# Spectral layer and MLP on one core: where the temporary of the last two conversion steps of w_in lies

## The chip, the cores and the metric

The kernel runs on one core of a Trainium2 chip. The metric is the device time of one execution in microseconds (us), the median of several runs. Before the change it is 2545.39 us, the median of 3 runs (2545.13 to 2547.89).

## The reference

Each of 8 sequences of 3008 tokens with 256 features is taken to the frequency domain, multiplied by a complex 256x256 matrix with a bias, soft-thresholded and taken back. The 24064 tokens that result go through an MLP with 2048 hidden features. The weights `w_in` and `w_out` come in float64.

```python
X = np.fft.rfft(x, axis=1)
Yr = Xr @ w_r - Xi @ w_i + b_r
Yi = Xr @ w_i + Xi @ w_r + b_i
Y = sign(Y) * maximum(abs(Y) - 0.01, 0)      # for Yr and Yi apart
x = np.fft.irfft(Yr + 1j * Yi, n=3008, axis=1)
h = x @ w_in
out = np.maximum(0.01 * h, h) @ w_out
```

## The kernel before, in words

The transform of 3008 points is split into 47 x 64. Four stages do the spectral layer of one sequence:

- `fwd` (stage A): the transform over 47. Its results go to DRAM (`u_dram`). For the second sequence its matmuls are `psh<-xin` (L310 to L311) and its copies `xin<-psh` (L313).
- `mid`: twelve rounds, one for each pair of rows of the first transform, called round 0 to round 11 below. A round loads `u` (L357), makes the transform over 64 (`stage_b`, PE `psh<-fb,u`, L371), copies it (ACT `ef<-psh`, L375; DVE adds real and imaginary part, L376), multiplies by the complex matrix in three products (`proj`: PE `pso<-w,ef` and `psf<-w,ef`), adds the bias (DVE `kb`, L409, and `t<-psf,kb`, L417), thresholds (DVE L418, L419), puts the halves in place (four ACT or DVE rows `zf<-t`, L423 to L427), transforms back over 64 (`stage_g`, PE `psh<-zf`, L442), copies (`v`, L450) and writes to DRAM (`v_dram`, L452).
- `inverse`: the transform back over 47. It loads the tile `vin` (tag `vin`, two slots of 240 KB loads in pairs, L495). Each of four calls for the first block of tokens (two pairs of sets x two halves of the features) makes four products into one of two PSUM banks `psf` (PE `psf<-ga,vin`, L516); ACT copies half of the result (`odd`, L519) and DVE makes the tokens (L520, L522), and ACT puts them in the token tile `yc` (L529).
- `forms` splits the tokens of a block of 512 into high and low parts (`yh`, `yl`, L542, L543) for fp32r products.

The MLP runs over 47 blocks of 512 tokens and 8 steps each: `psh<-yh,win` products (L98), a leaky ReLU, and `pso<-gh,wout` products (L644). From the first block's MLP on, the spectral stages of later sequences run between the MLP's matmuls. The prelude is what stands before that: stages A and mid of the first sequence, stage A of the second, the conversion of `w_in` and the start of that of `w_out`.

`convert_win(c)` turns one quarter of `w_in` from float64 into a high and a low fp32r part, with four sums for a Strassen form. `float64_parts` (L148) makes q and a from the raw words: ACT L153 writes `cvq`, ACT L154 writes `cva`, and DVE rows L155 to L159 finish the two; L184 adds them. L187 to L190 make the sums `ws`; ACT L193 and DVE L194 write `win_hi` and `win_lo` in three pieces each. The raw words of quarters 0 and 1 lie in the place of tag `wout_hi`, those of 2 and 3 in that of `wout_lo`, since `w_out`'s own tiles of these tags come only after the last quarter. The tiles `a`, `q`, `s` (`win_tmp`, L739 to L742) serve all four quarters; `a` is in a slot of tag `vin`, `q` of `gf`, `s` of `yh`.

A call of `convert_win` gives its instructions to a scheduler, which sets the order on each engine by a timeline of its own, within the `issue_after` ties that the code gives. Quarter 2 is converted after the third sixteenth of mid (L763), quarter 3 after the last threshold (L770). Each engine takes its instructions in the order that the scheduler wrote, and the SP queue likewise takes its DMA issues.

Of the kernel before, what the change touches and what calls it, by code (L numbers as in the profile page):

```python
# [8 lines left out]
F32 = mybir.dt.float32  # L9
# [11 lines left out]
P = 128  # L21
# [10 lines left out]
def spectral_mlp_kernel(  # L32
# [23 lines left out]
    NH = D // P  # L56
# [13 lines left out]
    sb = ctx.enter_context(tc.tile_pool(name="sb", bufs=2))  # L70
# [77 lines left out]
    def float64_parts(raw, a, q):  # L148


        wl, wh = raw[:, :, 0], raw[:, :, 1]
        u = a.bitcast(U32)
        act.mul(q, wl, 2.0 ** -52)  # L153
        act.activation(a, wh.bitcast(F32), AF.Abs, scale=2.0 ** 16)  # L154
        dve.tensor_scalar(a, a, F64_MIN * 2.0 ** 16, F64_MAX * 2.0 ** 16, ALU.max, ALU.min)  # L155
        dve.tensor_scalar(u, u, 4, 1, ALU.logical_shift_left, ALU.logical_shift_right)
        dve.scalar_tensor_tensor(u, wh, 0x80000000, u, ALU.bitwise_and, ALU.bitwise_or)
        dve.tensor_scalar(wl, u, 0xFF800000, None, ALU.bitwise_and)
        dve.tensor_mul(q, q, wl.bitcast(F32))  # L159
# [5 lines left out]
    NIN = DF // 4  # L165
# [13 lines left out]
    def convert_win(c):  # L179


        a, q, s = win_tmp
        float64_parts(win_raw[c], a, q)
        dve.tensor_add(a, a, q)  # L184
        a = a.rearrange("p (j q i m) -> p j q i m", j=NH, q=2, i=2)
        a11, a12, a21, a22 = (a[:, j, :, i] for i in range(2) for j in range(2))
        dve.tensor_add(s[:, 0], a21, a22)  # L187
        dve.tensor_sub(s[:, 2], a11, a21)
        dve.tensor_sub(s[:, 1], s[:, 0], a11)
        dve.tensor_sub(s[:, 3], a12, s[:, 1])  # L190
        hi, lo = (w[:, :, 2 * c:2 * c + 2] for w in consts["win"])
        for k, w in ((slice(0, 2), a[:, :, :, 0]), (2, a22), (slice(3, 7), s)):
            act.copy(hi[:, k], w)  # L193
            last = dve.tensor_sub(lo[:, k], w, hi[:, k].bitcast(F32))  # L194
        return last
# [528 lines left out]
    for h in range(2):  # L724
# [16 lines left out]
        sb.tile([P, NH * NIN], F32, name="cva", tag="vin"), sb.tile([P, NH * NIN], F32, name="cvq", tag="gf"),  # L741
        sb.tile([P, 4, 2, P], F32, name="ws", tag="yh"))  # L742
    convert_win(0)
    with tc.issue_after(turned[0].ins):
        split_consts()
# [12 lines left out]
    with tc.issue_after(turned[0].ins):  # L758
        convert_win(1)
    wout = load_wout()  # L760
    for i in range(1, 17):
        m0.to(i / 16)
        if i == 3:  # L763
            convert_win(2)
        if 5 <= i < 12:
            next(fp)
        if i == 13:
            next(wout)
# [146 lines left out]
```

## Time and profile before

| what | value |
|---|---|
| median of 3 runs | 2545.39 us (2545.13 to 2547.89) |
| the profiled execution | 2545.12 us, of which its span 2543.3 us |
| busy PE / DVE / ACT in the span | 98% / 74% / 66% |
| mean granted TensorE clock | 0.995 |
| first matmul of the MLP | 119.75 us from the span's start |

A row of the timeline gives the start and the length in us from the span's start, the engine, the line, output and input tiles, the shapes, and how many instructions are merged; the bracket says how long the engine sat idle before and what it waited for. One float32 product shows as two PE records. The length of a row is that of its results; the next row on an engine can start a little before it ends, so steps below are taken from start to start. SPq and ACTq rows are DMA issues.

### The profile page before, as it was taken

How to read it: one execution, taken by the hardware profiler on the slowest of the kernel's cores; microseconds unless marked ns; L12 is line 12 of the kernel's file. 1: busy time of each engine (PE TensorE's matmuls, PEld its weight loads, DVE VectorE, ACT ScalarE, POOL GpSimd, SP SyncE). 2: the span in 40 equal slices, each digit the busy share in tenths (PEclk: the TensorE clock that was granted, in tenths of full speed). 3: DMA queues.
4: the chain of work that ended last, by engine and by line, in shares of the span. 5: the costliest groups of instructions: out<-in, count | busy, mean ns of one | idle time of the engine just before them, and what ended most of it. 6: DMA issues, size and time to landing. Idle time of an engine off the chain costs nothing.

```text
span 2543.3 us, 42385 instructions
## 1 busy us (share of the span) xinstructions
PE 2500.5 (98%) x16180; PEld 2251.0 (89%) x16180; DVE 1877.5 (74%) x3460; ACT 1675.1 (66%) x3152; POOL 116.9 (5%) x96
## 2 busy tenths in 40 slices
PE   6999999999999999999999999999999999999999
PEld 4688889999899998999989999899998998999998
DVE  7887778777877778777786777877778776766675
ACT  4776756677666765677656677567765676666564
POOL 0000000000000000000000000000000000000000
PEclk8999999999999999999999999999999999999999
DMA  8621132111421113221141211411114111100000
GB/s 268 195 80 50 45 92 84 46 53 38 113 63 42 54 38 110 58 58 43 41 118 50 58 42 38 123 57 54 37 35 134 50 50 42 44 21 29 10 17 17
DMA packets 117803, 165.05 MB, mean 65 GB/s; under 512 B 13513, under 2 KB 69345, under 8 KB 117601
## 3 DMA queue, kind: packets, MB, share of 16 engines
q1 hardware_dynamic: 76228, 112.34, 14.5%
q10 hardware_dynamic: 41373, 50.01, 7.6%
q8 instruction: 127, 2.08, 0.3%
q14 instruction: 75, 0.61, 0.1%
HBM read 86.59 MB, written 75.71 MB: 64 GB/s over the span
## 4 chain that ended last, share of the span: by engine, by line
PE 92%; DVE 3%; DMA 2%; ACT 2%; issue 1%; ACTq 0%; SPq 0%; DVEq 0%
PE pso L644 39%; PE psh L98 35%; PE psf L84 11%; PE psf L516 4%; PE psf L371 3%; DMA xin<-x_dram 1%; DMA u_dram<-xin 1%; DVE gl L597 0%; PE psh L84 0%; PE psh L371 0%; PE pso L84 0%; DVE gf L628 0%; DMA win_raw<-w_in_dram 0%; DVE xz L279 0%; DMA vin<-v_dram 0%
## 5 line engine op out<-in xcount | busy, mean ns | idle before, releaser
L98 PE MATMUL psh<-yh,win_hi 128*128 128x256 f32 (+1 forms) x2608 | 736.5, 283 | 2.6 <-DVE gf L628 2.2
L98 PE MATMUL psh<-yl,win_hi 128*128 128x256 f32 (+1 forms) x2608 | 729.3, 280 | 0.0
L98 PE MATMUL psh<-yh,win_lo 128*128 128x256 f32 (+1 forms) x2608 | 726.6, 280 | 0.0
L597 DVE TENSOR_TENSOR gl<-gf,gh 128x1024 fp32r<-128x1024 f32 x376 | 460.8, 1226 | 323.8 <-ACT gh L595 315.8
L644 PE MATMUL pso<-gl,wout_hi 128*128 128x512 f32 x1504 | 590.6, 393 | 1.8 <-DVE gl L597 1.7
L644 PE MATMUL pso<-gh,wout_hi 128*128 128x512 f32 x1504 | 590.2, 392 | 1.1 <-ACT gh L595 1.1
L644 PE MATMUL pso<-gh,wout_lo 128*128 128x512 f32 x1504 | 589.7, 392 | 0.0
L98 PEld LDWEIGHTS psh<-yh,win_hi 128*128 128x128 f32 x2608 | 489.9, 188 | 20.5 <-DVE gf L628 4.6
L98 PEld LDWEIGHTS psh<-yl,win_hi 128*128 128x128 f32 x2608 | 491.0, 188 | 16.4 <-DVE yl L543 0.3
L98 PEld LDWEIGHTS psh<-yh,win_lo 128*128 128x128 f32 x2608 | 489.9, 188 | 2.1
L595 ACT CAST gh<-gf 128x1024 fp32r<-128x1024 f32 x376 | 394.8, 1050 | 43.7 <-PE pso L644 30.8
L631 ACT ACTIVATE gf<-gf 128x768 f32<-128x768 f32 x368 | 311.8, 847 | 153.7 <-DVE gf L628 140.3
L644 PEld LDWEIGHTS pso<-gl,wout_hi 128*128 128x128 f32 x1504 | 283.0, 188 | 61.7 <-DVE gl L597 3.8
L644 PEld LDWEIGHTS pso<-gh,wout_hi 128*128 128x128 f32 x1504 | 283.0, 188 | 46.3 <-ACT gh L595 1.9
L644 PEld LDWEIGHTS pso<-gh,wout_lo 128*128 128x128 f32 x1504 | 282.8, 188 | 45.5
L630 ACT ACTIVATE gf<-psh 128x256 f32<-128x256 f32 x368 | 142.2, 386 | 239.3 <-PE psh L98 233.5
L628 DVE TENSOR_TENSOR gf<-psh,u 128x512 f32<-128x512 f32 x368 | 252.0, 685 | 25.6 <-PE psh L98 24.1
L612 ACT COPY p<-psh 128x256 f32<-128x256 f32 x368 | 136.9, 372 | 147.5 <-PE psh L98 140.0
L409 POOL TENSOR_TENSOR kb<-bias,kc 128x512 f32<-128x512 f32 x84 | 114.3, 1360 | 2056.8 <-ACT kc L407 1804.2
L613 DVE TENSOR_TENSOR u<-psh,p 128x256 f32<-128x256 f32 x368 | 154.2, 419 | 70.6 <-ACT p L612 69.6
L615 DVE TENSOR_TENSOR gf<-psh,u 128x256 f32<-128x256 f32 x368 | 154.3, 419 | 29.3 <-PE psh L98 15.4
L616 DVE TENSOR_TENSOR gf<-psh,gf 128x256 f32<-128x256 f32 x368 | 154.1, 419 | 5.3
(124 smaller groups left out, 3153.5 us busy)
## 6 DMA issues: line engine op xcount, KB each, us to landing
u<-u_dram SPq DMA_DIRECT2D x192, 128.0 KB, 2.7
v_dram<-v ACTq DMA_DIRECT2D x192, 128.0 KB, 2.4
out_dram<-ob SPq DMA_DIRECT2D x94, 256.0 KB, 2.0
vin<-v_dram SPq DMA_DIRECT2D x96, 240.0 KB, 3.6
xin<-x_dram SPq DMA_DIRECT2D x78, 240.0 KB, 3.0
u_dram<-xin ACTq DMA_DIRECT2D x72, 240.0 KB, 2.4
raw<-w_out_dram SPq DMA_DIRECT2D x8, 512.0 KB, 4.8
win_raw<-w_in_dram SPq DMA_DIRECT2D x7, 512.0 KB, 6.8
```

The lines of the kernel that those rows point to most:

```text
L84: last = nc.tensor.matmul(dst, a, b, start=(i == 0), stop=(i == len(terms) - 1))
L98: mlp[:] = [nc.tensor.matmul(dst, a, b, start=start and i == 0, stop=i == 2, skip_group_check=True)]
L595: cp = act.copy(gh, g)
L597: parted[:] = [cp, dve.tensor_sub(gl, g, gh.bitcast(F32))]
L612: act.copy(p1, b1[:, lo])
L613: dve.tensor_add(u2, b1[:, hi], p1)
L615: dve.tensor_add(g[:, 3], b2[:, hi], u2)
L616: dve.tensor_add(g[:, 3], b2[:, lo], g[:, 3])
L628: dve.tensor_add(g[:, 1:3], b2.rearrange("p (k n) -> p k n", k=2), u2.unsqueeze(1).broadcast_to([P, 2, HT]))
L630: act.activation(g[:, 0], b1[:, lo], AF.Prelu, alpha=SLOPE)
L631: act.activation(g[:, 1:4], g[:, 1:4], AF.Prelu, alpha=SLOPE)
L644: mlp[:] = [nc.tensor.matmul(po, a[:, f, s], r[:, i], start=(f == 0 and j == 0), stop=(f == NF - 1 and j == 2),)]
```

## The change

For quarters 2 and 3 the temporary `a` is a new tile in the place of tag `wout_hi`, which held the raw words of quarters 0 and 1. The slot of tag `vin` holds `a` for quarters 0 and 1 only.

```diff
         a, q, s = win_tmp
+        if c >= 2:
+            a = sb.tile([P, NH * NIN], F32, name="cva", tag="wout_hi", bufs=1)
         float64_parts(win_raw[c], a, q)
```

No instruction is added or removed, but the scheduler puts many in another order. All lines below L181 have two more in the changed kernel (L371 is L373 there). The number behind a name tells tiles of one name apart.

On PE, in mid, after the third round's product with the sum (`pso_345`, round 2), before:

```order
L84 MATMUL pso_345<-w32_105,ef_229 128x256 x2
L84 MATMUL psf_346<-w32_105,ef_229 128x256 x4
L371 MATMUL psh_338<-fb_103,u_277 128x2x64 x4
L84 MATMUL psh_382<-zf_230,w32_105 128x512
L371 MATMUL psh_391<-fb_103,u_306 128x2x64 x4
L84 MATMUL psf_399<-w32_105,ef_229 128x256 x4
L84 MATMUL pso_398<-w32_105,ef_229 128x256 x2
L84 MATMUL psh_417<-zf_230,w32_105 128x512
```

The same place now:

```order
L84 MATMUL pso_345<-w32_105,ef_229 128x256 x2
L373 MATMUL psh_338<-fb_103,u_277 128x2x64 x4
L84 MATMUL psf_346<-w32_105,ef_229 128x256 x4
L84 MATMUL pso_399<-w32_105,ef_229 128x256 x2
L84 MATMUL psf_400<-w32_105,ef_229 128x256 x4
L84 MATMUL psh_383<-zf_230,w32_105 128x512
L373 MATMUL psh_392<-fb_103,u_306 128x2x64 x4
L84 MATMUL psh_418<-zf_230,w32_105 128x512
```

The transform of round 3 (`psh_338`) has moved ahead of the `psf` products of round 2, and both projections of round 3 ahead of the first `psh<-zf`.

On DVE, at the same time, between quarter 1's sums and the second `t` row (`t_297` is round 0, `t_326` round 1, `cva_180` the old temporary), before:

```order
L417 TENSOR_TENSOR t_297<-psf_288,kb_291 128x512
L194 TENSOR_TENSOR win_lo_179<-cva_180,win_hi_178 128x2x256
L194 TENSOR_TENSOR win_lo_179<-cva_180,win_hi_178 128x256
L189 TENSOR_TENSOR ws_182<-ws_182,cva_180 128x256
L418 TENSOR_SCALAR c_298<-t_297 128x512
L409 TENSOR_TENSOR kb_320<-bias_248,pso_316 128x512
L190 TENSOR_TENSOR ws_182<-cva_180,ws_182 128x256
L419 TENSOR_TENSOR t_297<-t_297,c_298 128x512
L417 TENSOR_TENSOR t_326<-psf_317,kb_320 128x512
```

And now (`cva_351` is the new temporary, quarter 2):

```order
L155 TENSOR_SCALAR cva_351<-cva_351 128x1024
L419 TENSOR_TENSOR t_297<-psf_288,kb_291 128x512
L196 TENSOR_TENSOR win_lo_179<-cva_180,win_hi_178 128x2x256
L196 TENSOR_TENSOR win_lo_179<-cva_180,win_hi_178 128x256
L191 TENSOR_TENSOR ws_182<-ws_182,cva_180 128x256
L156 TENSOR_SCALAR cva_351<-cva_351 128x1024
L420 TENSOR_SCALAR c_298<-t_297 128x512
L411 TENSOR_TENSOR kb_320<-bias_248,pso_316 128x512
L192 TENSOR_TENSOR ws_182<-cva_180,ws_182 128x256
L378 TENSOR_TENSOR ef_229<-ef_229 128x2x128
L157 SCALAR_TENSOR_TENSOR cva_351<-win_raw_251,cva_351 128x1024
L421 TENSOR_TENSOR t_297<-t_297,c_298 128x512
```

Three rows of quarter 2 and round 3's `ef` row have come ahead of round 0's threshold row (L419 before, L421 now). On ACT, `cva<-win_raw_251` of quarter 2 (L154) now stands directly behind round 2's `ef` copy, ahead of quarter 1's `win_hi` casts; before it came after all three of these.

On ACT, where the last of the four inverse calls is read out (`odd_828` before), before:

```order
L313 COPY xin_557<-psh_835 96x512
L529 COPY yc_797<-y_818 128x470
L519 COPY odd_828<-psf_823 128x240
L313 COPY xin_557<-psh_838 96x512
L313 COPY xin_557<-psh_841 96x512
```

And now (`odd_830`):

```order
L315 COPY xin_558<-psh_837 96x512
L315 COPY xin_558<-psh_840 96x512
L531 COPY yc_799<-y_820 128x470
L521 COPY odd_830<-psf_825 128x240
L315 COPY xin_558<-psh_843 96x512
```

The last `odd` row has gone from behind one to behind two of the three last copies of stage A.

On the SP queue, the four `vin` loads of the first block stood in the order pair 0, 0, 1, 1; now it is 0, 1, 0, 1, followed as before by two loads of `w_out`.

## The prediction

> **What bounds the kernel now.** I read the page first, then the busy time by stretches.
>
> ```profile
> span 2543.3 us, 42385 instructions
> PE 2500.5 (98%) x16180; PEld 2251.0 (89%) x16180; DVE 1877.5 (74%) x3460; ACT 1675.1 (66%) x3152; POOL 116.9 (5%) x96
> PE 92%; DVE 3%; DMA 2%; ACT 2%; issue 1%; ACTq 0%; SPq 0%; DVEq 0%
> ...
> 160.00:2543.00 2383.00, 2368.31 (x15649) 2157.21 (x15647) 1751.54 (x3244) 1569.77 (x2957) 116.11 (x90) 1.00 0.20 56
> ```
>
> PE bounds it: 42.8 us of the span are idle on PE, and only 14.7 of these come after 160 us. The other 28 lie in the prelude, which is what the change touches. After the prelude a shift of PE's start is carried to the end, since PE has next to no idle time there to take it up.
>
> The timeline of PE in mid, where the order changes, comes next:
>
> ```profile
> 48.18 1.89 PE L84 MATMUL psf<-w,ef 128*128 128x256 f32 x8
> 50.94 1.16 PE L371 MATMUL psh<-fb,u 128*128 128x128 f32 x8 [0.87 <-DMA u<-u_dram]
> 53.69 1.13 PE L84 MATMUL psh<-zf,w 128*128 128x512 f32 x2 [1.60 <-ACT zf L427]
> ...
> 55.55 1.89 PE L84 MATMUL psf<-w,ef 128*128 128x256 f32 x8
> 57.28 1.03 PE L84 MATMUL pso<-w,ef 128*128 128x256 f32 x4
> 58.14 1.02 PE L84 MATMUL psh<-zf,w 128*128 128x512 f32 x2
> 59.00 1.05 PE L371 MATMUL psh<-fb,u 128*128 128x128 f32 x8
> ...
> 67.27 1.10 PE L84 MATMUL pso<-w,ef 128*128 128x256 f32 x4 [1.15 <-DVE ef L376]
> ```
>
> Round 3's transform (50.94) waits for its load of `u`. While that load is on its way PE does round 2's `psf` products (48.18). The other two waits are for ACT and DVE, which are both full here. DVE and then ACT over the same time:
>
> ```profile
> 46.54 0.68 DVE L417 TENSOR_TENSOR t<-psf,kb 128x512 f32<-128x512 f32 x1
> ...
> 49.68 0.68 DVE L419 TENSOR_TENSOR t<-t,c 128x512 f32<-128x512 f32 x1
> 50.28 0.68 DVE L417 TENSOR_TENSOR t<-psf,kb 128x512 f32<-128x512 f32 x1
> ...
> 53.55 0.68 DVE L419 TENSOR_TENSOR t<-t,c 128x512 f32<-128x512 f32 x1
> ...
> 54.75 0.68 DVE L156 TENSOR_SCALAR cva<-cva 128x1024 uint32<-128x1024 uint32 x1
> 55.35 0.41 DVE L376 TENSOR_TENSOR ef<-ef 128x256 f32<-128x256 f32 x1
> ...
> 56.02 1.21 DVE L157 SCALAR_TENSOR_TENSOR cva<-win_raw,cva 128x1024 uint32<-128x1024 uint32 x1
> ...
> 58.09 0.69 DVE L158 TENSOR_SCALAR win_raw<-cva 128x1024 uint32<-128x1024 uint32 x1
> ```
>
> ```profile
> 45.84 1.17 ACT L153 ACTIVATE cvq<-win_raw 128x1024 f32<-128x1024 uint32 x1 [0.37 <-DMA win_raw<-w_in_dram]
> ...
> 50.74 1.16 ACT L154 ACTIVATE cva<-win_raw 128x1024 f32<-128x1024 f32 x1
> 51.80 0.39 ACT L423 COPY zf<-t 64x256 f32<-64x256 f32 x1
> ...
> 53.14 0.50 ACT L427 ACTIVATE zf<-t,sign 64x256 f32<-64x256 f32 x1
> 53.67 0.59 ACT L375 COPY ef<-psh 128x512 f32<-128x512 f32 x1
> ```
>
> The raw words of quarter 2 land at 45.84. Last, the SP queue's waits and issues, and the end of the prelude on PE and ACT:
>
> ```profile
> SPq L495 <- DVE win_lo L194: 3.6, 1, 3.6
> ```
>
> ```profile
> 103.25 0.82 SPq L495 DMA_DIRECT2D vin<-v_dram  x2
> 107.68 0.77 SPq L495 DMA_DIRECT2D vin<-v_dram  x2
> ```
>
> ```profile
> 97.73 1.10 PE L84 MATMUL psh<-zf,w 128*128 128x512 f32 x2 [0.23 <-DVE zf L425]
> ...
> 109.94 1.05 PE L516 MATMUL psf<-ga,vin 120*128 120x128 f32 x8
> 112.51 0.68 PE L516 MATMUL psf<-ga,vin 120*128 120x128 f32 x4 [1.51 <-DMA vin<-v_dram]
> 113.59 4.10 PE L516 MATMUL psf<-ga,vin 120*128 120x128 f32 x20 [0.40 <-DMA vin<-v_dram]
> ...
> 122.08 1.02 PE L98 MATMUL psh<-yh,win_hi 128*128 128x512 f32 x2 [0.38 <-ACT yh L542]
> ```
>
> ```profile
> 118.63 0.58 ACT L313 COPY xin<-psh 96x512 f32<-96x512 f32 x1 [1.69 <-PE psh L84]
> ...
> 119.60 0.35 ACT L519 COPY odd<-psf 128x240 f32<-128x240 f32 x1
> ```
>
> Pair 1's loads waited 3.6 us for quarter 3's last read of the old temporary, and PE 1.9 us for them. The MLP runs without a break from 122.08 on.
>
> **The change part by part.** *The wait that it removes.* Pair 1's slot is now free when quarter 1 is done, long before 100 us. So all four loads go out together. What can be won is bounded by the 1.9 us of PE's waits and the slow matmuls behind them: 20 inverse records took 4.10 us at 113.59, where 8 took 1.05 at 109.94, so some 2.1 us were lost. Bounds of this term: 0 to -4.0 us.
>
> *The order of mid.* The load that ends at 50.94 and the landing at 45.84 are set by the queue of DMAs, whose order on SP is as before up to there. I work the new order out from the rows, with each instruction starting when the one ahead lets go and its inputs are there.
>
> DVE: the new first row, L155 of quarter 2, needs ACT's L154, which needs the landing: 45.84 + 1.16 = 47.0. L155 lets go after 0.6 (L156's 54.75 to 55.35), so `t` of round 0 starts at 47.6, not 46.54. The rows up to L419 take 3.1 as before (46.54 to 49.68), and L156 adds 0.6: DVE stands at 51.3 before round 3's `ef` row, which now comes first.
>
> PE: round 3's transform starts at 50.94 as before, but nothing fills the time from 48.18: the hole is 2.8, not 0.9. It ends at 52.1; ACT copies 0.6; DVE's `ef` runs at 52.7 after 1.4 idle, L157 adds 1.1, and round 0's threshold row starts at 54.2, 4.5 later than 49.68. The four `zf` rows (1.84, from 51.80 to 53.64) end at 56.8.
>
> PE meanwhile does round 2's `psf` (51.8 to 53.6), round 3's `pso` (to 54.4), and must wait for a bank of `psf` that `t` of round 1 empties (54.8 to 55.5), so round 3's `psf` runs from 55.5 to 57.2 (1.73 from 55.55 to 57.28), the first `psh<-zf` to 58.1, round 4's transform to 59.0. The second `psh<-zf` needs round 1's threshold. From `t` to that row DVE took 3.27 (50.28 to 53.55); without L155 (0.6), with L158 and L159 (0.6 and 1.1) it is 4.4: 59.2. With its own 0.7 and four `zf` rows it is 61.8 to 62.0. PE waits 3.0 us, and round 5's transform starts at 62.9 instead of 59.00. The same work is done on PE at both points: **+3.9 us**.
>
> Behind it, the wait of 1.15 at 67.27 can go, as DVE has more lead over PE: at least +2.7 is left. But when quarter 2's last row leaves DVE, four rounds have had their `t` row and not five, so rounds come later to ACT. The same bookkeeping continued to the last `psh<-zf` finds further waits for `zf` of 1.3, 0.8 and 1.0 and gives 103.4 for 97.73 (for the old order it gives 97.5). I take **+5.7**, between +2.7 and +6.5.
>
> *The loads at their new place.* They go out at 103.25 + 5.7 = 109.0, and the last lands 5.9 later by the slowest row (107.68 to 113.59): 114.9. The first inverse starts at 109.94 + 5.7 = 115.6, or 116.1, as the conversion's ACT rows now stand ahead of some `xin` copies. So PE no longer waits for `vin`. What is late next: there are two `psf` banks, and the third call waits until the first has been read by one ACT and two DVE rows. It starts at 118.6, the fourth at 120.4. Then the last three `psh<-xin` run, and ACT's last `odd` row stands behind two of their copies and not one (118.63, 119.60). The second of these products ends at 123.1, the `odd` row runs at 124.2, and 2.5 us from it to the MLP (119.60 to 122.08), or 3.1 with the third copy, make 126.7 to 127.3. That is 11 us after the first inverse against 12.1: of the 4.0 to be won the read-out leaves 1.1 at most, and 0.5 of it is lost ahead. I take **-0.4**, between -2 and +0.5.
>
> *The clock.* Stretches of 3.41 us, on the boundaries at which the granted clock changes (the second number is PE's busy time, the third from the end the granted clock):
>
> ```profile
> 49.33:52.74 3.41, 1.90 (x12) 1.28 (x10) 3.41 (x7) 2.92 (x5) 0.00 (x0) 1.00 0.42 114
> 110.77:114.18 3.41, 1.50 (x12) 1.14 (x11) 2.45 (x6) 2.04 (x5) 0.00 (x0) 1.00 0.80 267
> 114.18:117.59 3.41, 3.41 (x19) 3.41 (x18) 2.77 (x7) 2.46 (x6) 0.00 (x0) 0.51 1.04 414
> ```
>
> A stretch with 1.50 us of PE work was followed by one at half clock, one with 1.90 was not. The new waits of 3.0 at 59 and of some 2.6 ahead of 127 can each leave a stretch with less than 1.5, and a stretch at half clock loses up to 1.7 us; the old one at 114 goes or stays. I take **+0.7**, between -1 and +3.4.
>
> The Trainium skill ("TensorE: Matmul & The Clock Gate", Part 1) puts the fall to half rate behind at least one idle window of about 3.4 us. By that rule neither new wait would cost clock and the sum would be 0.7 less; the trace agrees on the window's length but not on the idle: 1.50 us of work in a window did not keep the clock up.
>
> *Without a price:* `w_out`'s high part takes the place of the new temporary, but its first cast stands behind quarter 3's casts on ACT in both orders. The amount of work is the same on every engine. The later order differs too, and I know no sign for it: -3 to +3.
>
> The sum is 5.7 - 0.4 + 0.7 = +6.0 on the profiled execution's own 2545.12 us (span 2543.3 and 1.8 around it; the median of the runs is 0.27 above it): **2551.1 us**.
>
> **The rivals.** *Only the wait goes* (faster side): the `u` load or quarter 2 lands some 3 us sooner than in the trace, so that the new order costs nothing, and the read-out keeps pace. Then 2545.1 - 4.0 = 2541.1. For it: the scheduler chose this order by a timeline on which it paid. Against it: both landings are in rows, and no DMA ahead of them moves. It decides where the load of round 3 is there by 48.2.
>
> *Only the first hole counts:* PE packs from 63 us on, +2.7 - 0.4 = +2.3, 2547.4. It needs DVE and ACT to make up the lost round before PE has used up its own work; that mid's later rounds showed no PE wait between 68 and 95 us in the old order speaks for it, that the new order puts the `zf` products close behind their thresholds speaks against it.
>
> *Late waits vanish:* two waits behind the prelude were
>
> ```profile
> 359.58 0.47 PE L84 MATMUL psf<-xz,fa_hi 120*120 120x512 f32 x1 [1.77 <-ACT ob L649]
> ```
>
> ```profile
> 2129.71 0.50 PE L644 MATMUL pso<-gh,wout_hi 128*128 128x512 f32 x1 [1.07 <-ACT gh L595]
> ```
>
> With a half-clock stretch of 1.7 behind each they are worth 6.2; in the new order both could go: 2551.1 - 6.2 = 2544.9.
>
> *More of the same:* both new waits and one late one each bring a stretch at half clock: 6.0 - 0.7 + 3 x 1.7 = +10.4, 2555.5.
>
> That the change doesn't do what it says is excluded: on SP the loads of pair 1 stand between those of pair 0 now.
>
> **How the numbers follow.** Forecast 0.62 (own range 2547.5 to 2555), only the wait goes 0.13, only the first hole 0.10, late waits vanish 0.07, more of the same 0.08. A change of 0.2% (5.1 us) is about what a measurement of this kernel can tell from none; from the median that is 2540.3 and 2550.5. Of the forecast's 0.62, 0.40 lie above 2550.5, with 0.08 of the last case: slower 0.48. Faster has 0.05, from the first and third rival at their best. The rest is 0.47. The range of 2543 to 2556 leaves out most of the first rival and the tails above.
>
> **What would show it.** Right: on PE a hole of 2.8 us ahead of round 3's transform and one of about 3 ahead of the second `psh<-zf`; the last `psh<-zf` at 103 to 104 us; no wait for `vin`; `psh<-yh` without a break from 127 to 128.5. Wrong: the second `psh<-zf` before 60 us, or the last before 99.

## The result and the profile after

| | before | changed |
|---|---|---|
| median | 2545.13 us (2540.35 to 2547.89) | 2556.66 us (2555.18 to 2558.7) |
| ratio | 1 | 1.0051 (95%: 1.004 to 1.0061) |
| profiled execution | 2545.12 us, span 2543.3 | 2558.7 us, span 2556.9 |

The kernel became 11.5 us slower. The forecast was 6.0 us slower, 2551.1; the range ended at 2556, 0.7 us too low.

The busy time by stretches comes first, cut at the same pieces of work in both kernels: first transform of mid, last `psh<-zf`, first `psh<-yh`, and the 418th, 626th, 1878th and last record of `psh<-yh`. The columns are from:to, length, busy PE, PEld, DVE, ACT and POOL, the granted clock, and the DMA share and GB/s. Before:

```profile
36.46:98.24 61.78, 57.66 (x268) 45.72 (x268) 52.02 (x90) 42.55 (x82) 0.00 (x0) 0.95 0.69 194
98.24:119.75 21.51, 18.68 (x63) 9.66 (x61) 18.27 (x33) 15.37 (x32) 0.00 (x0) 0.92 0.84 267
119.75:342.95 223.20, 220.00 (x1403) 197.34 (x1402) 167.44 (x309) 158.69 (x312) 17.01 (x13) 1.00 0.21 58
342.95:446.05 103.10, 101.06 (x635) 89.94 (x634) 82.70 (x155) 62.95 (x120) 2.58 (x2) 0.98 0.34 101
446.05:1030.85 584.80, 583.08 (x3865) 531.72 (x3864) 441.09 (x822) 391.48 (x743) 29.57 (x24) 1.00 0.22 63
1030.85:2532.38 1501.53, 1497.72 (x9905) 1365.87 (x9904) 1092.22 (x2015) 985.06 (x1837) 66.94 (x51) 1.00 0.18 50
```

The changed kernel:

```profile
35.88:107.25 71.37, 61.42 (x267) 47.87 (x268) 52.80 (x92) 43.00 (x83) 0.00 (x0) 0.90 0.61 168
107.25:128.23 20.98, 18.50 (x62) 8.70 (x61) 16.73 (x31) 15.36 (x31) 0.00 (x0) 0.92 0.86 278
128.23:352.76 224.53, 220.48 (x1391) 197.72 (x1390) 170.28 (x310) 158.67 (x309) 17.14 (x13) 0.98 0.20 57
352.76:462.78 110.02, 104.36 (x646) 92.46 (x645) 83.59 (x157) 65.84 (x122) 3.02 (x2) 0.95 0.33 95
462.78:1046.06 583.28, 582.77 (x3866) 531.82 (x3865) 440.54 (x822) 391.11 (x743) 29.52 (x24) 1.00 0.22 63
1046.06:2545.91 1499.85, 1496.36 (x9905) 1364.12 (x9904) 1092.86 (x2015) 984.24 (x1837) 66.87 (x51) 1.00 0.17 51
```

Length less length gives the bill: mid +9.6, read-out (the row from the last `psh<-zf` to the first `psh<-yh`) -0.5, the MLP up to the 418th record +1.3, **the stretch behind it +6.9**, the rest -1.5 and -1.7; mid itself began 0.6 sooner. That is 13.5 us for these two executions; the medians differ by 11.5. Length less busy is PE's idle time: 4.1 to 10.0 in mid and 2.0 to 5.7 in the fourth stretch. What is left of mid's loss is clock: busy time grew by 3.8 for the same work, at a granted clock of 0.90 for 0.95. In the fourth stretch it grew by 3.3, at 0.95 for 0.98.

PE's timeline of the changed kernel in the prelude:

```profile
50.51 2.07 PE L373 MATMUL psh<-fb,u 128*128 128x128 f32 x8 [3.96 <-DMA u<-u_dram]
...
63.72 2.08 PE L84 MATMUL psh<-zf,w 128*128 128x512 f32 x2 [3.06 <-DMA v_dram<-v]
...
106.72 1.12 PE L84 MATMUL psh<-zf,w 128*128 128x512 f32 x2
...
120.89 2.18 PE L518 MATMUL psf<-ga,vin 120*128 120x128 f32 x16
...
131.41 1.02 PE L98 MATMUL psh<-yh,win_hi 128*128 128x512 f32 x2 [1.23 <-ACT yh L544]
```

The row of ACT that ends the second wait, whatever releaser the bracket names:

```profile
63.16 0.50 ACT L429 ACTIVATE zf<-t,sign 64x256 f32<-64x256 f32 x1
```

Both forecast waits are there, and no inverse waits for `vin`. The last `psh<-zf` comes at 106.72 where 103 to 104 was forecast, and `psh<-yh` runs without a break from 131.41 where 127 to 128.5 was. The transform at 50.51 takes 2.07 us, where before it took 1.16: it runs at half clock. The stretches on the clock's boundaries show why:

```profile
46.30:49.72 3.42, 0.24 (x2) 0.00 (x0) 3.22 (x7) 2.02 (x4) 0.00 (x0) 1.00 0.99 214
49.72:53.13 3.41, 2.62 (x10) 2.53 (x11) 1.22 (x3) 0.46 (x1) 0.00 (x0) 0.50 0.26 63
53.13:56.54 3.41, 3.41 (x9) 2.69 (x9) 3.25 (x5) 2.10 (x5) 0.00 (x0) 0.50 0.60 155
59.96:63.37 3.41, 0.69 (x7) 0.50 (x5) 3.41 (x6) 1.95 (x5) 0.00 (x0) 1.00 0.57 174
63.37:66.79 3.42, 3.07 (x8) 2.04 (x9) 3.42 (x9) 3.36 (x7) 0.00 (x0) 0.51 0.52 147
```

Behind each wait the clock halves, for two stretches and for one. Half of PE's busy time in the three is (2.62 + 3.41 + 3.07) / 2 = 4.6 us.

The second loss lies where PE goes from batch 1 to batch 2 (a batch is a sequence, counted from 0). `psf<-zh,gb` is the transform back over 64 in mid, and `psf<-xz,fa` the transform over 47 that begins the next batch. PE, SP and DVE of the changed kernel:

```profile
364.78 0.40 PE L84 MATMUL psf<-zh,gb_lo 128*128 128x512 f32 x1
368.42 1.44 PE L84 MATMUL psf<-xz,fa_hi 120*120 120x512 f32 x3 [2.33 <-DVE xz L280]
...
376.04 1.63 PE L84 MATMUL psf<-xz,fa_hi 120*120 120x512 f32 x2 [3.15 <-DVE xz L280]
```

```profile
360.64 0.37 SPq L264 DMA_DIRECT2D xin<-x_dram  x1
368.25 0.32 SPq L503 DMA_DIRECT2D vin<-v_dram  x1
...
369.53 0.41 SPq L264 DMA_DIRECT2D xin<-x_dram  x1
```

```profile
366.01 0.69 DVE L630 TENSOR_TENSOR gf<-psh,u 128x512 f32<-128x512 f32 x1 [0.28 <-PE psh L98]
366.62 0.68 DVE L271 TENSOR_TENSOR xs<-xin,xin 120x512 f32<-120x512 f32 x1
...
374.13 0.69 DVE L271 TENSOR_TENSOR xs<-xin,xin 120x512 f32<-120x512 f32 x1 [4.23 <-DMA xin<-x_dram]
```

364.78 is batch 1's last product with `gb`. The two waits for `xz` behind it differ. For the first, 2.33 us, no load is late: its `xin` went out at 360.64, the loads and stores of this tile take at most 4.5 us here, and DVE comes to `xs` at 366.62 directly behind a row of the MLP. PE has only little work between and gets there before DVE has made `xz`. The second, 3.15 us, is for a load: the result of the last `gb` product goes to DRAM as `v`, SP's load of `vin` waits 7.2 us for that (3.2 before), the next `xin` goes out behind it at 369.53, and DVE waits 4.23 us for it. Before, the same rows stood wider apart:

```profile
347.67 0.40 PE L84 MATMUL psf<-zh,gb_lo 128*128 128x512 f32 x1
...
354.15 0.40 PE L84 MATMUL psf<-xz,fa_hi 120*120 120x512 f32 x1
```

```profile
352.96 0.41 SPq L262 DMA_DIRECT2D xin<-x_dram  x1
```

From the last `gb` product to the point at which PE stands ready for the first `xz` product are 6.5 us here (347.67 to 354.15), and 1.3 in the changed kernel (364.78 to 368.42 - 2.33).

### The profile page after: what moved, and what is told of

The parts are those of the page before. It is cut to its first block, busy times and chain, and to the rows that moved or that the text cites. A ratio compares the mean times of both kernels' runs of the same rounds, so it can differ in the third digit from the quotient of the medians.

```text
span 2556.9 us, 42397 instructions
## 1 busy us (share of the span) xinstructions
PE 2506.2 (98%) x16180; PEld 2253.3 (88%) x16180; DVE 1880.3 (74%) x3460; ACT 1676.7 (66%) x3152; POOL 117.3 (5%) x96
## 4 chain that ended last, share of the span: by engine, by line
PE 91%; DMA 3%; ACT 2%; DVE 2%; issue 1%; ACTq 1%; SPq 0%; POOL 0%; DVEq 0%; POOLq 0%
PE pso L646 39%; PE psh L98 34%; PE psf L84 11%; PE psf L518 3%; PE psf L373 3%; DMA xin<-x_dram 1%; DMA v_dram<-v 1%; DMA u_dram<-xin 0%; ACTq L454 0%; DVE gl L599 0%; PE psh L84 0%; ACT zf L429 0%; DMA u<-u_dram 0%; ACT v L452 0%; ACT zf L425 0%
```

## The experiments

The theory to begin with was the prediction's: the new order of mid makes the loss. Rivals: the place of the temporary itself, and the new order behind the prelude. Times are medians, with the ratio to the kernel before on the same chip (its medians there: 2541.65 for e1 to e4, 2542.99 for e5 to e8, 2542.92 for e9 to e12).

| run | edit | us | ratio, 95% |
|---|---|---|---|
| e1 | quarter 3's temporary alone moved | 2552.01 | 1.0039 (1.0027 to 1.0052) |
| e2 | quarter 2's alone moved | 2550.91 | 1.0038 (1.0025 to 1.005) |
| e3 | change, quarter 2 tied behind quarter 1 | 2551.31 | 1.0039 (1.0025 to 1.0053) |
| e4 | change, quarter 3's raw loads later | 2555.47 | 1.0054 (1.0041 to 1.0066) |
| e5 | e3, straddling `vin` loads on GpSimd | 2551.4 | 1.0028 (1.0017 to 1.0039) |
| e6 | change, idle products in the two waits | 2555.53 | 1.0049 (1.0037 to 1.0062) |
| e7 | the change again | 2553.89 | 1.0044 (1.0031 to 1.0057) |
| e8 | before again, one run | 2543.4 | |
| e9 | before, batch 1 paced later | 2548.17 | 1.0021 (1.0012 to 1.003) |
| e10 | before, paced later yet, distance kept | 2539.53 | 0.999 (0.9981 to 0.9999) |
| e11 | change, batch 1 paced earlier | 2543.99 | 1.0008 (1.0 to 1.0017) |
| e12 | e3, batch 1 paced earlier | 2537.14 | 0.9977 (0.9968 to 0.9986) |

**e1 and e2: one quarter each.**

```
-        if c >= 2:
+        if c >= 3:      # e1
+        if c == 2:      # e2
```

> Only quarter 3's temporary is in w_out's place; quarter 2's is back in the old slot. On PE the order of mid is the old one but for one product of psf, the later order is near the changed kernel's, and pair 1's slot is free early. Theory (the new order of mid makes the loss): last psh<-zf at 97 to 99 us as before, no wait for vin, first psh<-yh up to 4 us sooner than before, the later order's own loss 0 to 4.3: 2541 to 2549 us, likeliest 2546. Rival 1 (the temporary's place and the early free slot make the loss, whatever the order): 2553 to 2557. Rival 2 (the later order sets the end, the prelude's shift is taken up behind): 2549 to 2553.

> Only quarter 2's temporary is in w_out's place; quarter 3's is back in the old slot, so pair 1's loads wait for it again. On PE mid has a new order (round 3's transform ahead of round 2's psf, as in the changed kernel), and everything behind mid is in the order of before. Theory (the new order of mid makes the loss): last psh<-zf at 103 to 108 us for 97.73 before, the vin wait is kept, and the shift at the end is the same as at the first psh<-yh, +9 to +13: 2554 to 2558 us. Rival 1 (place and free slot): 2543 to 2548. Rival 2 (the later order sets the end): 2545 to 2549.

Each half alone made the kernel slower by nearly as much as the whole change. e2 has the new order of mid and keeps the later order of before; its mid, and the fourth stretch, which lost nothing:

```profile
36.44:105.04 68.60, 59.87 (x267) 47.44 (x268) 53.02 (x91) 42.06 (x81) 0.00 (x0) 0.92 0.63 177
...
350.38:451.70 101.32, 99.42 (x635) 88.75 (x633) 82.44 (x155) 62.83 (x120) 2.59 (x2) 1.00 0.35 102
```

So mid's new order alone costs: 68.60 for 61.78. The time of e2 lies between the ranges of the theory and of the second rival. e1 has the old order of mid, but for one product, and the new one behind. Its fourth stretch took 109.18 us, 6.1 more than before, and its time lies where the second rival put it. But its mid took 65.86 us in the profiled execution, with nearly the old order: round 3's `u` was there only at 53.26, and behind that wait of 2.85 us two stretches ran at half clock. So part of this execution's loss is a late load, not the order. There are two losses, not one, and the medians of the halves don't add up to that of the whole: +10.4 and +9.3 us against +11.5. Why not is open.

**e3: the old order of mid within the change.**

```
-        convert_win(1)
+        done1 = convert_win(1)
...
-            convert_win(2)
+            with tc.issue_after(done1.ins):
+                convert_win(2)
```

> The whole change, with the conversion of quarter 2 held behind the last instruction of quarter 1, which is where the old slot held it. On PE mid has nearly the old order, the later order is near the changed kernel's. Theory (the new order of mid makes the loss): round 3's transform waits under 1.5 us, last psh<-zf at 97 to 99.5, no wait for vin, first psh<-yh 0 to 4 us sooner than before, the later order's own loss 0 to 4.3: 2541 to 2549 us. Rival 1 (place and free slot): 2553 to 2557. Rival 2 (the later order sets the end): 2549 to 2553.

```profile
36.77:99.22 62.45, 58.00 (x267) 45.41 (x268) 51.93 (x90) 42.61 (x82) 0.00 (x0) 0.95 0.68 192
99.22:118.30 19.08, 17.23 (x62) 8.08 (x61) 17.50 (x32) 15.04 (x31) 0.00 (x0) 1.00 0.86 288
...
340.14:450.55 110.41, 104.09 (x647) 91.98 (x645) 83.54 (x157) 65.34 (x122) 3.03 (x2) 0.97 0.33 95
```

Mid is back at its old length, the read-out is 2.4 us shorter without the wait for `vin`, and 7.3 us are lost behind. The prelude went as the theory said, and the sum did not: the rival of the later order holds.

**e4: the hole ahead of round 3's transform.**

```
-    for c in range(2, 4):
-        load_win(c, (sync, sync), reads[3])
+    load_win(2, (sync, sync), reads[3])
...
         m0.to(i / 16)
+        if i == 2:
+            load_win(3, (sync, sync), reads[-1])
```

> The whole change, with the two raw loads of quarter 3 issued on SP behind round 3's loads of u and not ahead of them. The order of PE differs from the changed kernel's in a few rows of mid alone. Theory (the hole ahead of round 3's transform is its load behind four raw loads of 512 KB, and it pushes all of mid): two such loads at the 400 GB/s of this stretch are 2.6 us, so u lands at about 48, the hole is 1 to 1.5 us for 3.96, the last psh<-zf is at 102 to 104.5 for 106.72: 2551 to 2555 us. Rival (the chain of DVE and ACT through quarter 2's conversion sets the second psh<-zf, and the hole only lies beside it): the wait for zf grows by what the hole loses, last psh<-zf at 106 to 107: 2556 to 2557.

```profile
49.85 1.13 PE L373 MATMUL psh<-fb,u 128*128 128x128 f32 x8 [3.00 <-DMA u<-u_dram]
...
63.98 1.24 PE L84 MATMUL psh<-zf,w 128*128 128x512 f32 x2 [3.73 <-DMA v_dram<-v]
```

`u` landed 0.7 us sooner and not 2.6, and what the hole lost, the wait for `zf` gained: 3.00 + 3.73 for 3.96 + 3.06. As the rival had it, the chain through DVE and ACT sets the second `psh<-zf` (63.98 for 63.72). The last one came at 105.83 and the time is 2555.47, both between the two ranges. Why the load came so little sooner is open.

**e5: the loads of `xin` and `vin` apart.**

```
-                sync.dma_start(vin[:, c, i, :], vv[c, :, s_, :])
+                pool.dma_start(vin[:, c, i, :], vv[c, :, s_, :])
```

> The tied kernel (quarter 2's conversion held behind quarter 1) with the loads of vin that straddle two batches issued by GpSimd instead of SP, so that batch 2's second xin load no longer stands behind one of them. PE's order is the tied kernel's up to 370 us but for a few rows. Its profile lost 7.3 us between 343 and 446 us against before: 4.3 of PE idle, 1.5 of half clock, 1.5 of slower products. Theory (the later order brings batch 1's last product for v some 4.5 us later, SP's load of vin waits 7.2 us for it, and the load of xin behind it is late): xin goes out some 4 us sooner, PE's second wait for xz (2.61) is under 0.8, and 2.5 to 5 us come back: 2546 to 2549 us. Rival (DVE's and PE's new order alone makes those waits, the load is not the cause): the second wait stays above 2, 2550 to 2553 us.

```profile
359.68 1.72 PE L84 MATMUL psf<-xz,fa_hi 120*120 120x512 f32 x3 [2.33 <-DVE xz L280]
363.77 1.22 PE L518 MATMUL psf<-ga,vin 120*128 120x128 f32 x4 [0.48 <-DMA vin<-v_dram]
366.97 0.80 PE L518 MATMUL psf<-ga,vin 120*128 120x128 f32 x2 [1.97 <-DMA vin<-v_dram]
```

The second wait for `xz` went, and waits for `vin` took its place. `xin` still went out late, at 360.17, behind another load of `vin`. Inconclusive: the queue isn't shown to be the cause.

**e6: products that nobody reads in the two new waits.**

```
+            for _ in range(14 if b == 0 and j == 3 else 0):
+                nc.tensor.matmul(pb[:, :D], consts["wr32"][0][:, 0, :P], consts["wr32"][0][:, 0, :], start=True, stop=True)
...
+            for _ in range(12 if b == 0 and j == 1 else 0):
+                nc.tensor.matmul(pg[:, :D], consts["wr32"][0][:, 0, :P], consts["wr32"][0][:, 0, :], start=True, stop=True)
```

> The whole change, with products that nobody reads (128x256, some 0.22 us each) put ahead of round 3's transform (14) and ahead of the second psh<-zf (12), in the banks that those write anyway. They keep PE busy in its two new waits; the order of the later rounds and behind mid is another one again. Theory (the new waits let the clock fall, and half of the prelude's loss is clock): no stretch at half clock between 45 and 70 us, where the change had three worth some 4.6 us, and from the first transform to the last psh<-zf 66 to 69 us for 71.4: 2551 to 2555 us. Rival (DVE and ACT set the rounds, so that a slower PE costs nothing there): the stretches go, but 70 to 72 us stay: 2555 to 2558 us.

```profile
49.36 4.91 PE L370 MATMUL psh<-w 128*128 128x256 f32 x22
54.11 1.05 PE L375 MATMUL psh<-fb,u 128*128 128x128 f32 x8
```

There was no stretch at half clock between 43 and 309 us: with PE kept busy in the two waits, the clock stayed up. But a product took 0.43 us and not 0.22, so the 26 of them are 11 us of work for 7 of waiting, and mid stayed at 70.9 us. What the clock alone is worth doesn't come out of it.

**e7 and e8: both kernels again on one chip.** No edit.

> The changed kernel once more, on the same chip as the others. Theory (PE's waits set where the clock falls): stretches at half clock right behind the waits ahead of round 3's transform, of the second psh<-zf, and of xz near 370 us, and waits and clock as in the first profile within 2 us; last psh<-zf at 104 to 107: 2553 to 2557 us. Rival (the stretches come on their own and made the first profile long): they lie elsewhere, and last psh<-zf at 99 to 103: 2547 to 2552 us.

> The kernel before once more, for its trace on the same chip. Theory: at most two stretches at half clock behind 50 us, near 114 and 360 us, last psh<-zf at 96 to 99, 2539 to 2545 us. Rival (the first profile was a chance case): the waits and stretches of the changed kernel appear here too, last psh<-zf above 101.

The changed kernel:

```profile
37.00:107.17 70.17, 61.19 (x267) 47.84 (x268) 52.53 (x91) 41.96 (x81) 0.00 (x0) 0.90 0.59 171
107.17:126.87 19.70, 17.11 (x63) 8.17 (x61) 16.74 (x31) 15.27 (x31) 0.00 (x0) 1.00 0.88 286
126.87:348.73 221.86, 217.80 (x1392) 195.68 (x1391) 170.16 (x310) 158.20 (x309) 17.14 (x13) 1.00 0.21 59
348.73:458.09 109.36, 103.93 (x646) 92.22 (x645) 83.28 (x157) 65.73 (x122) 3.03 (x2) 0.97 0.33 96
```

The kernel before:

```profile
37.02:98.80 61.78, 58.10 (x268) 45.72 (x269) 52.08 (x90) 42.08 (x82) 0.00 (x0) 0.95 0.70 194
98.80:120.56 21.76, 18.66 (x63) 9.65 (x61) 18.26 (x33) 15.46 (x32) 0.00 (x0) 0.92 0.84 264
120.56:343.77 223.21, 220.02 (x1403) 197.34 (x1402) 167.47 (x309) 158.78 (x312) 17.00 (x13) 1.00 0.21 58
343.77:446.58 102.81, 100.82 (x635) 89.91 (x634) 82.66 (x155) 62.95 (x120) 2.58 (x2) 0.98 0.35 101
```

The two waits (4.21 and 3.05 us) and the half-clock stretches behind them are there again, and in e8 they are not. On one chip the prelude is worth +8.4 - 2.1 = +6.3 us, and what follows up to the 626th record -1.4 + 6.6 = +5.2.

**e9 to e12: the distance.** In the program's order 54 units of MLP work (128x256 products, 0.116 us each) stand on PE between batch 1's last `gb` product and batch 2's first `xz` product before (60 up to the second, which the expectation of e9 gives), and 8 in the changed kernel. One number of the pacing, which says how far the spectral instructions must have got at each step of the MLP, sets it:

```
-        work = frac / 0.95 * sum(s.total for s in streams)
+        work = frac / (0.97 if cur == 0 else 0.95) * sum(s.total for s in streams)    # e9; 0.98 in e10, 0.91 in e11 and e12
```

> The kernel before, with batch 1's spectral stage paced a little later (0.97 for 0.95). On PE the only change of note is behind the prelude: between the last gb product of batch 1 and the first xz product of batch 2 stand 9 units of work of the MLP (128x256 products, 0.116 us each: 1.0 us), where the kernel before has 60 (6.9 us) and the changed kernel 8 (0.9 us). Theory (the later order loses at 340 to 380 us because that product has moved against its readers' neighbours, so that vin, xin and with them xz come late): PE waits of above 2 us for xz near 360 and 370 us, 4 to 6 us lost there: 2546 to 2549 us. Rival (the distance doesn't matter; other parts of the later order lose): no new wait there, 2541 to 2544 us.

> The kernel before with the same pacing at 0.98. As many rows move as at 0.97, but the distance between batch 1's last gb product and the first xz product stays at 54 units (6.2 us). Theory (the distance decides): no wait for xz above 1 us, 2541 to 2545 us. Rival (any new order of this stretch loses): 2546 to 2549 us.

> The whole change, with batch 1's spectral stage paced a little earlier (0.91 for 0.95). The prelude's order is the changed kernel's; the distance between batch 1's last gb product and the first xz product is 72 units (8.3 us) for 8. Theory: the waits for xz go, and of the stretch's 6.6 us 4 to 6 come back; the prelude's 6 us stay: 2547 to 2550 us. Rival (the distance doesn't matter): 2552 to 2555 us.

> The tied kernel (quarter 2's conversion held behind quarter 1) with the pacing of 0.91; distance 72 units for 8. Both losses are then undone and the gain of the early vin loads is kept. Theory: 4 to 6 us below the tied kernel's 2551.3: 2544 to 2547 us, and if all of the vin gain comes through, 2540 to 2543, below the kernel before. Rival (the distance doesn't matter): 2550 to 2553 us.

e9, the kernel before with the short distance:

```profile
357.39 0.40 PE L84 MATMUL psf<-zh,gb_lo 128*128 128x512 f32 x1
361.66 1.72 PE L84 MATMUL psf<-xz,fa_hi 120*120 120x512 f32 x3 [2.82 <-DVE xz L278]
...
368.16 0.75 PE L84 MATMUL psf<-xz,fa_hi 120*120 120x512 f32 x1 [1.60 <-DVE xz L278]
```

The changed kernel's waits appear in the kernel before, with its loss: 5.3 us by the medians, and 107.47 us for the fourth stretch. With as many rows moved but the distance kept (e10) nothing is lost, 3.4 us are even won. e12's fourth stretch:

```profile
341.17:440.80 99.63, 98.75 (x634) 88.79 (x633) 81.01 (x154) 63.37 (x118) 3.02 (x2) 1.00 0.35 102
```

It has 0.9 us of idle PE and no half clock. Over all 14 traces the fourth stretch took 99.6 to 103.1 us where the distance is 54 or 72 units (six traces), and 107.5 to 113.5 us where it is 8 or 9 (eight traces). The distance is the cause of the second loss. Within its chain it stays open which link binds: DVE's rows ahead of the first `xz`, the load of `vin` on SP, or the slot that `xin` is loaded into.

The size of the loss is less sure than its cause. Each taken against the kernel before on its own chip, e11 lies 9.8 us below e7 and e12 15.4 us below e3, more than the 5.3 us of e9, and e10, e11 and e12 all came out 1.5 to 3 us below the ranges expected. So the pacing brings something besides the distance, and what that is stays open.

e10, e11 and e12 ran side by side, all with the long distance, so they price the prelude. The old order of mid is worth 2543.99 - 2537.14 = 6.9 us (e11 against e12, which differ in the tie alone). The early `vin` loads are worth 2539.53 - 2537.14 = 2.4, and the change as a whole 2543.99 - 2539.53 = +4.5; these two compare kernels of different pacing, 0.98 in e10 and 0.91 in the others. e12 beats both kernels: 5.8 us below before.

## Why the prediction failed, by its steps

- *PE-bound, a shift is carried to the end.* Right: past the 626th record the two profiles of e7 and e8 differ by -1.4 and +0.2 us more.
- *The wait that it removes, and the read-out: -0.4.* The wait is gone in the first profile, and in e7 0.43 us of it is left. Side by side the read-out gained 2.1 us (e7, e8) or 2.4 (e12 against e10), because the half-clock stretch behind the old wait goes as well; in the first pair another one took its place (0.92 in both second rows) and the gain was 0.5. The bound of 4.0 was too wide: from the rows that the prediction shows, the slow matmuls lost 4.10 - 20 x 1.05 / 8 = 1.5 us, not 2.1.
- *The order of mid: +5.7.* Right in place and cause (e2, e3). The hole was forecast at 2.8 and is 3.96, since PE was ahead; the second `psh<-zf` waits 3.06 for the forecast 3.0. Idle PE in mid grew by 5.8 us; that the last `psh<-zf` came 9.0 us later and not 5.7 is the clock.
- *The clock: +0.7.* The term was too small by some 2.6 for mid: each of the two waits brought half clock, 4.6 us in three stretches, against 1.3 that the early stretch of before costs mid more (it lasted to 42.5 us there and to 39.4 in the changed kernel).
- *The later order, "I know no sign for it: -3 to +3", taken as 0.* **This step failed.** It is +5.2 side by side, and about as much in every kernel with the new later order (e1, e3, e4: 6.1 to 7.3 in the fourth stretch). The program's order showed where to look: the last `gb` product of batch 1 had moved from 54 to 8 units ahead of batch 2's first `xz` product. The prediction followed the order through the prelude and no further; that the short distance costs time was shown by e9 to e12.
- *The rivals.* "Only the wait goes" is what e12 does, by another way: it needs the old order of mid and the long distance. "More of the same" gave 2555.5 and was nearest to the time. Its half clock behind both new waits is there, but it has nothing for the new waits for `xz`, so that it came so near is luck.

The sum for the prelude, +6.0, stands against +6.3 in one pair of profiles, +8.5 in the other and +4.5 by e10 and e11. The time was missed mostly by what came after it.

## What to carry to other kernels

A buffer that is freed earlier also frees a scheduler to reorder: price each stretch that it reorders, far behind the edit too, by the distance between a producer's last product and the first consumer of the slots and data that it releases. If the freed wait is wanted and the new order isn't, tie the moved step where the old wait held it, and look at the distances again.

## What the runs showed of the hardware

A clock stretch of 3.41 us needs no full idle to let the clock fall. Over all traces of this case, from 45 us to 20 us before the end, each of the 31 full-clock stretches in which PE was busy for less than 1.67 us was followed by one at half clock. None with more than 2.34 us was, and between the two both occur (7 fell, 49 did not). In the last 20 us two with some 1.5 us of work did not fall (2537.69 before, 2540.97 in e3), so the amount of work is not all that decides. The Trainium skill ("TensorE: Matmul & The Clock Gate", Part 1) names at least one idle window; in these 31 stretches PE was busy up to 1.66 us and the clock fell all the same.

One wait can cost more than one stretch: the 3.96 us ahead of the transform at 50.51 brought two in a row, and its last 0.8 us lay in the first of them, in which PE was busy for 2.62 us. From 45 us on, each of the 12 half-clock stretches with up to 2.81 us of PE work was followed by another, and none of the 37 with 2.99 us or more was.
